# Zero-padded k^T scores, packed kv transposes, and q transposed by VectorE in a fused linear-attention and expert-attention kernel

## The chip, the cores and the metric

The kernel runs on one core of a Trainium2 chip. A core has a matrix engine (TensorE, PE in the profile, its weight loads shown as PEld), a vector engine (VectorE, DVE), a scalar engine (ScalarE, ACT), GpSimd (POOL) and an engine that here only issues transfers (SyncE, SP), beside 16 DMA engines. Each engine runs its own instructions in order and waits on semaphores. The metric is the device time of one execution in microseconds; lower is better.

## The reference

Two layers, batch 8, 8 heads, sequence 576, head size 64, all float32. The first is attention without softmax, and a norm over each head:

```python
kv = np.einsum('bhsd,bhse->bhde', k, v)
out = np.einsum('bhsd,bhde->bhse', q, kv)
rms = np.sqrt(np.mean(out * out, axis=-1, keepdims=True) + 1e-06)
out / rms * g_norm            # heads side by side give x: (8, 576, 512)
```

The second has four experts, each a causal softmax attention with head size 64; every token takes the two experts with the largest logits:

```python
logits = x @ w_gate           # two largest, softmax over the two -> w
for e in range(4):
    q, k, v = x @ wq[e], x @ wk[e], x @ wv[e]
    a = causal_softmax(q @ k.transpose(0, 2, 1) / 8)
    out += (w of e, where e is among the two) * (a @ v @ wo[e])
```

## The kernel before

Each batch passes through three generators, and a planner's loop (`merge`, L517) writes their pieces into one program in the order of estimated costs (`yield 4.3` and the like, with totals `CA, CX, CS`, L526).

**`stage_a(b)` (L191), the first layer.** `p_kv` gathers k^T v of all heads, two heads in the two halves of the partitions, over four blocks of 128 positions and a rest of 64. `kv_copy` writes it to `kvx` (the two heads beside each other, on the diagonal) and to `kv2` (the same as a full 128x128 block with zeros). `p_kt` transposes the four blocks of `kv2`; `p_kg` multiplies them with the gate weights (`wg_bd`), which gives four further columns of `kvx`, so that the logits come out beside the attention output. `q_block(i)` (L196) turns block i of q (128 positions, 8 heads) into `qT`, with four TensorE transposes into PSUM (`p_q`, L200) and one VectorE copy (L205); there are five blocks, the last with 64 positions. `p_out` (L242) then multiplies qT with kvx, block by block. VectorE copies it to `o_sb` (L249), ScalarE squares it (L253), VectorE sums the squares (L259). A chain of small VectorE operations makes the inverse root (L270 to L282), and POOL scales the rows into `x_tok` (L297).

**`stage_x(b)` (L307)** transposes x_tok on TensorE (`p_x`) and ScalarE copies it to `xT`.

**`stage_s(b)` (L323), the second layer.** VectorE makes the gates. `proj(pr)` makes q^T and k^T of two experts at a time, one in partitions 0 to 63, the other in 64 to 127 (`qTp` and `kT`, one ScalarE copy each, L384); `kT` rotates through three tiles whose columns 576 to 639 are zero. `scores(pr)` multiplies, for each block of keys and each of the two experts (`el`), the 64 rows of that expert (L400); ScalarE takes the exponential into `PT` (L410), POOL masks the diagonal blocks (L415). `pv(pr)` multiplies with v, `o_t` transposes, and `final` (L502) makes the output rows, which SyncE stores (L512). The order within the stage is a written string (L494 to L496).

**Order.** Stage A of batch 0 comes first, then stage X of 0 beside stage A of 1, then for each b stage S of b beside stage X of b+1 and stage A of b+2. The framework then orders each engine's instructions by this program order and by its own estimate of when operands are ready, so an instruction can move ahead of an earlier one that isn't ready.

**Loads.** `load_qkv` (L110) fetches one batch on SyncE's queue: k and v in runs of 1 KB, their rests and q in runs of 256 bytes; q comes last, one transfer per block (L134). Two batches fit (`bufs=2`). The weights (L158) pass through one staging tile and a VectorE scaling each (L159). Stores are on the same queue.

## Time and profile before

| | |
|---|---|
| time, median of 3 runs | 328.2 us (323.96 to 330.56) |
| the profiled execution's own time | 324.47 us |
| its span in the profile | 322.5 us |
| mean granted TensorE clock | 0.945 |
| busy: PE, DVE, ACT, POOL | 276.0, 189.2, 153.0, 79.5 us |
| DMA queue | 75248 packets, 39.86 MB, 47.1% of 16 engines' span |

Busy time of TensorE counts overlapping matmuls once; the ends of matmuls are modelled, so starts are the better measure of what one costs. A row of the groups names line, engine, operation, the tile written and those read, then for matmuls the active rows and columns of the array (64*128 is a matmul over 64 rows). The chain of work follows the last instruction back to what released it, step by step. A row of the stages gives the busy time of each engine between two times of the span. In the timeline a row is a run of like instructions: its start, its length to the end of the last one, and their number.

### The profile page before, as it was taken

The page shows a single profiled execution, that of the slowest core. Times are in us where ns is not written, and L with a number is a line of the kernel's source. Part 1 is how long each engine was busy: PE and PEld are TensorE (multiplying, and loading weights), DVE is VectorE, ACT ScalarE, POOL GpSimd, SP SyncE. Part 2 cuts the span into 40 slices and gives each one's busy share as a digit, 9 for nine tenths or more (in the row PEclk, how much of TensorE's full clock was granted, in tenths as well). Part 3 has the DMA queues.
Part 4 walks back from the last instruction along what each step waited for, and adds up shares of the span by engine and source line. Part 5 has one row for each costly group of instructions (what it writes and reads, how often), then busy time and mean ns, then how long its engine had stood idle before and what let it go on. Part 6 is the DMA issues. An engine that isn't in the chain of part 4 may idle for free.

```text
span 322.5 us, 6704 instructions
## 1 busy us (share of the span) xinstructions
PE 276.0 (86%) x2624; PEld 220.4 (68%) x2624; DVE 189.2 (59%) x537; ACT 153.0 (47%) x273; POOL 79.5 (25%) x148
## 2 busy tenths in 40 slices
PE   1675579799979997999889996999889996999984
PEld 1565468588858775887667875887667875867641
DVE  0249948846884568646775578546774578424130
ACT  0203123653464654545554554545555554585843
POOL 8100600441044110702053101612052101630210
PEclk9959599999999999799999999799999999899977
DMA  6977999999704269194608372001200120021124
GB/s 195 243 199 195 205 301 223 298 180 276 152 2 133 64 202 192 41 253 127 169 3 269 81 182 58 2 0 67 82 2 2 65 83 0 0 100 53 65 83 147
DMA packets 75280, 40.30 MB, mean 125 GB/s; under 512 B 54000, under 2 KB 70384, under 8 KB 75248
## 3 DMA queue, kind: packets, MB, share of 16 engines
q1 hardware_dynamic: 75248, 39.86, 47.1%
q8 instruction: 21, 0.34, 0.5%
q14 instruction: 11, 0.09, 0.1%
HBM read 30.42 MB, written 9.44 MB: 124 GB/s over the span
## 4 chain that ended last, share of the span: by engine, by line
PE 70%; DVE 10%; ACT 9%; SPq 4%; issue 3%; POOL 1%; DMA 1%; DVEq 0%; ACTq 0%; POOLq 0%
PE p_proj L373 11%; PE p_out L242 11%; PE p_v L355 7%; PE p_sc L400 7%; PE p_O L451 7%; PE p_y L506 6%; PE p_q L200 6%; PE p_x L313 6%; PE p_kv L179 5%; ACT PT L410 3%; PE p_kg L224 3%; DVE o_sb L249 3%; SPq L134 2%; PE p_OT L484 2%; POOL x_tok L297 1%
## 5 line engine op out<-in xcount | busy, mean ns | idle before, releaser
L415 POOL TENSOR_SCALAR_AFFINE_SELECT PT<-PT 128x256 bf16<-128x256 bf16 (+1 forms) x80 | 29.3, 381 | 143.4 <-ACT PT L410 143.4
L410 ACT ACTIVATE PT<-p_sc 128x576 bf16<-128x576 f32 (+3 forms) x80 | 53.9, 714 | 20.1 <-PE p_sc L400 18.1
L297 POOL TENSOR_TENSOR x_tok<-o_sb,y 128x512 f32<-128x512 f32 (+1 forms) x40 | 42.0, 1080 | 85.1 <-DVE y L280 85.0
L242 PE MATMUL p_out<-kvx,qT 128*128 128x136 f32 (+1 forms) x320 | 48.1, 292 | 0.0
L400 PE MATMUL p_sc<-qTp,kT 64*128 64x288 f32 (+2 forms) x192 | 35.7, 358 | 10.7 <-ACT PT L410 5.9
L242 PEld LDWEIGHTS p_out<-kvx,qT 128*128 128x128 f32 (+1 forms) x320 | 40.2, 181 | 4.8 <-ACT sq L253 2.1
L253 ACT ACTIVATE sq<-p_out 128x512 f32<-128x512 f32 (+1 forms) x40 | 23.8, 596 | 39.9 <-DVE o_sb L249 38.4
L318 ACT CAST xT<-p_x 128x512 fp32r<-128x512 f32 (+1 forms) x40 | 21.8, 545 | 34.3 <-PE p_x L313 34.3
L400 PEld LDWEIGHTS p_sc<-qTp,kT 64*128 64x128 f32 x192 | 19.8, 185 | 21.9 <-ACT PT L410 8.5
L179 PE MATMUL p_kv<-v_b,k_b 128*64 128x64 f32 x512 | 25.7, 260 | 10.3 <-DMA v_b<-in_v_dram 10.3
L249 DVE COPY o_sb<-p_out 128x544 f32<-128x544 f32 (+1 forms) x40 | 28.7, 719 | 7.7 <-PE p_out L242 7.2
L362 DVE CAST vext<-p_v 128x256 bf16<-128x256 f32 (+1 forms) x40 | 17.0, 425 | 26.3 <-PE p_v L355 25.6
L259 DVE TENSOR_REDUCE ms<-sq 128x8 f32<-128x520 f32 (+1 forms) x40 | 27.4, 688 | 7.9 <-ACT sq L253 7.8
L205 DVE COPY qT<-p_q 128x512 f32<-128x512 f32 (+1 forms) x40 | 24.7, 634 | 11.6 <-PE p_q L200 11.0
L451 PEld LDWEIGHTS <-PT 128*128 128x128 bf16 (+2 forms) x480 | 24.1, 103 | 10.8 <-issue 5.3
L179 PEld LDWEIGHTS p_kv<-v_b,k_b 128*64 128x64 f32 x512 | 23.0, 173 | 12.2 <-DMA k_b<-in_k_dram 6.7
L451 PE MATMUL p_O<-vext,PT 128*128 128x65 bf16 (+2 forms) x480 | 30.3, 199 | 0.4 <-ACT PT L410 0.4
L313 PE MATMUL p_x<-ident_f,x_tok 128*128 128x128 f32 (+1 forms) x160 | 25.9, 289 | 5.4 <-POOL x_tok L297 4.3
L355 PE MATMUL p_v<-wv_r,xT 128*128 128x256 f32 (+1 forms) x160 | 28.3, 300 | 0.7 <-ACT kv L188 0.7
L373 PE MATMUL p_proj<-xT,wk_r 128*128 128x288 f32 x128 | 24.3, 314 | 3.6 <-ACT qTp L384 3.6
L506 PE MATMUL p_y<-wo_b,OT 128*128 128x512 bf16 (+1 forms) x80 | 25.1, 417 | 0.7 <-ACT OT L489 0.7
L511 ACT COPY y<-p_y 128x512 f32<-128x512 f32 (+1 forms) x40 | 23.0, 595 | 5.0 <-PE p_y L506 2.7
(67 smaller groups left out, 360.9 us busy)
## 6 DMA issues: line engine op xcount, KB each, us to landing
q_b<-in_q_dram SPq DMA_DIRECT2D x32, 256.0 KB, 5.2
out_dram<-y SPq DMA_DIRECT2D x32, 256.0 KB, 2.1
k_b<-in_k_dram SPq DMA_DIRECT2D x7, 1024.0 KB, 6.0
v_b<-in_v_dram SPq DMA_DIRECT2D x7, 1024.0 KB, 10.2
k_b<-in_k_dram SPq DMA_DIRECT2D x4, 256.0 KB, 4.7
v_b<-in_v_dram SPq DMA_DIRECT2D x4, 256.0 KB, 4.9
k_rem<-in_k_dram SPq DMA_DIRECT2D x8, 128.0 KB, 9.2
v_rem<-in_v_dram SPq DMA_DIRECT2D x8, 128.0 KB, 7.5
```

Source lines behind the costliest of these rows:

```text
L179: nc.tensor.matmul(p_kv[hh * Dh : (hh + 1) * Dh, c, :], lhsT=lk, rhs=rv, start=(j == 0), stop=(j == NF), skip_group_check=True,)
L242: nc.tensor.matmul(p_o[:nt, c // 2, (c % 2) * 2 * GW : (c % 2 + 1) * 2 * GW], lhsT=qT[:, c, t0 : t0 + nt], rhs=kvb[:, c, :, :].rearrange(" ...
L249: nc.vector.tensor_copy(out=ob[:nt, i].rearrange("p (k h) g -> p k (h g)", k=2), in_=p_o[:nt, :, 0 : 4 * GW])
L297: nc.gpsimd.tensor_tensor(out=xt[:nt], in0=ob[:nt, i, :, 0:Dh], in1=y[:nt, i * H : (i + 1) * H].unsqueeze(2).to_broadcast([nt, H, Dh]), op ...
L313: nc.tensor.transpose(p_x[:, c, :nt], xts[i][:nt, 2 * c : 2 * c + 2, :].rearrange("p h d -> p (h d)"), ident_f[:nt, :nt],)
L355: nc.tensor.matmul(p_v[:nt, :], lhsT=xT[:, c, t0 : t0 + nt], rhs=w_r["v"][:, c, :, :].rearrange("p e f -> p (e f)"), start=(c == 0), stop= ...
L373: nc.tensor.matmul(p_p[:, s, 0:HALF], lhsT=w_r[nm][:, c, 2 * pr : 2 * pr + 2, :].rearrange("p e f -> p (e f)"), rhs=xT[:, c, s * HALF : (s ...
L400: nc.tensor.matmul(p_s[:, el, o : o + hi - lo], lhsT=kTp[pb, kb * P : (kb + 1) * P], rhs=qTp[pb, lo:hi], start=True, stop=True,)
L410: nc.scalar.activation(PT[:, :, d0 : d0 + o], p_s[:, :, 0:o], ACTF.Exp, scale=scale)
L415: nc.gpsimd.affine_select(out=d, in_=d, compare_op=AluOpType.is_ge, fill=0.0, base=0, pattern=[[0, 2], [1, w]], channel_multiplier=-1,)
L451: nc.tensor.matmul(p_O[:nq, bank, (2 * n + el) * (Hd + 1) : (2 * n + el + 1) * (Hd + 1)], lhsT=PT[:nk, el, col : col + nq], rhs=vx[:nk, kb ...
L506: nc.tensor.matmul(p_y[:nq, :], lhsT=OT[:, pr, s0 : s0 + nq], rhs=wo_b[:, pr, :], start=(pr == 0), stop=(pr == EP - 1),)
```

## The change

1. **Scores.** Each pair of experts gets two `kT` tiles instead of one, `kT{pr}{el}`. The 64 partitions of the other expert and the columns past 576 are set to zero once. ScalarE copies k^T in two pieces, one to each tile, and the score matmul runs over all 128 rows with the whole `qTp`. The tiles of a pair are used again in each batch.
2. **Packed kv.** ScalarE copies `p_kv` as it is to `kvc`, with four 64-column pieces side by side; two of them make one 128x128 transpose, so there are two transposes and two `p_kg` products a batch. `wg_bd` is laid out to match, loaded in four transfers, and the result goes to `kvx` in two copies.
3. **q.** The load puts 32 dimensions of one head on 32 partitions, each position's 32 values a run of 128 bytes: 16 transfers a batch instead of 5. Four VectorE transposes of 32x32 blocks, one for each pair of heads, then make `qT` at the start of stage A. `q_block` and `p_q` are gone.
4. **Start.** The weights come in the order q, k, v, staged in the buffers of x_tok; wo is staged in those of y. Stage X of batch 0 runs alone, stage S of 0 beside stage A of 1, then stage X of 1 beside stage A of 2; from batch 1 on the streams are as before. The load of batch 3 is issued after the first of these. The planner's totals and yields are changed.

```diff
-        t = const.tile([P, NCH, P], FP32, name=f"kv2_{j}")
-        nc.gpsimd.memset(t[:], 0.0)
-        kv2s.append(t)
+        t = const.tile([P, NCH, Dh], FP32, name=f"kvc{j}")
...
+    zrow = ysb.tile([P, NB * P], FP32, tag="zrow", name="zrow", bufs=1)
+    nc.gpsimd.memset(zrow[:], 0.0)
...
+    kTs = []
+    for pr in range(EP):
+        pair = []
+        for el in range(2):
+            t = const.tile([P, NB * P], FP32R, name=f"kT{pr}{el}")
+            other = slice((1 - el) * Hd, (2 - el) * Hd)
+            nc.vector.tensor_copy(out=t[other, :], in_=zrow[other, :])
+            nc.vector.tensor_copy(out=t[:, S : NB * P], in_=zrow[:, S : NB * P])
+            pair.append(t)
+        kTs.append(pair)
...
-        qt = qkvp.tile([P, NB, H, Dh], FP32, tag="q_b", name="q_b")
+        qt = qkvp.tile([P, NCH, S // 32, 32], FP32, tag="q_b", name="q_b")
...
-        for i, (t0, nt) in enumerate(blocks):
-            nc.sync.dma_start(
-                qt[:nt, i, :, :], q[b, :, t0 : t0 + nt, :].rearrange("h p d -> p h d")
-            )
+        for c in range(NCH):
+            for hh in range(2):
+                for dh in range(2):
+                    p0 = (2 * hh + dh) * 32
+                    nc.sync.dma_start(
+                        qt[p0 : p0 + 32, c, :, :],
+                        q[b, 2 * c + hh, :, dh * 32 : (dh + 1) * 32].rearrange("(g p) d -> p g d", p=32),
+                    )
         return qt, kt, vt
...
-    wg_st = const.tile([P, NCH, E], FP32, name="wg_st")
-    nc.sync.dma_start(wg_st[:], moe_w_gate.rearrange("(c p) e -> p c e", p=P))
-    wg_bd = const.tile([P, NCH, 2, E], FP32, name="wg_bd")
+    wg_st = const.tile([P, EP, 2, E], FP32, name="wg_st")
+    for c2 in range(2):
+        for m in range(EP):
+            h0 = 4 * m + 2 * c2
+            nc.sync.dma_start(
+                wg_st[c2 * Dh : (c2 + 1) * Dh, m, :, :],
+                moe_w_gate[h0 * Dh : (h0 + 2) * Dh, :].rearrange("(a d) e -> d a e", d=Dh),
+            )
+    wg_bd = const.tile([P, EP, 2, 2, E], FP32, name="wg_bd")
     nc.gpsimd.memset(wg_bd[:], 0.0)
-    for hh in range(2):
-        pp = slice(hh * Dh, (hh + 1) * Dh)
+    for c2 in range(2):
+        pp = slice(c2 * Dh, (c2 + 1) * Dh)
         nc.vector.tensor_scalar_mul(
-            out=wg_bd[pp, :, hh, :], in0=wg_st[pp], scalar1=g_wide[pp]
+            out=wg_bd[pp, :, c2, :, :], in0=wg_st[pp], scalar1=g_wide[pp]
         )
     w_r = {}
-    for name, wdram in (("v", moe_wv), ("q", moe_wq), ("k", moe_wk)):
+    for name, wdram in (("q", moe_wq), ("k", moe_wk), ("v", moe_wv)):
         wr = const.tile([P, NCH, E, Hd], FP32R, name=f"w{name}_r")
-        wf = wst.tile([P, NCH, E, Hd], FP32, name="w_stage", tag="w_stage")
-        for e in range(E):
-            nc.sync.dma_start(wf[:, :, e, :], wdram[e].rearrange("(c p) f -> p c f", p=P))
-        nc.vector.tensor_scalar_mul(
-            out=wr[:].rearrange("p c e f -> p (c e f)"),
-            in0=wf[:].rearrange("p c e f -> p (c e f)"),
-            scalar1=g_wide[:],
-        )
+        for c0 in range(0, NCH, 2):
+            wf = blk.tile([P, 2, E, Hd], FP32, tag="x_tok", name="w_stage", bufs=NB + 1)
+            for c in range(2):
+                nc.sync.dma_start(
+                    wf[:, c, :, :],
+                    wdram[:, (c0 + c) * P : (c0 + c + 1) * P, :].rearrange("e p f -> p e f"),
+                )
+            nc.vector.tensor_scalar_mul(
+                out=wr[:, c0 : c0 + 2].rearrange("p c e f -> p (c e f)"),
+                in0=wf[:].rearrange("p c e f -> p (c e f)"),
+                scalar1=g_wide[:],
+            )
         w_r[name] = wr
     loads[1] = load_qkv(1)
-    wo_st = wst.tile([P, EP, D], FP32, name="wo_st", tag="w_stage")
+    wo_b = const.tile([P, EP, D], BF16, name="wo_b")
     for pr in range(EP):
-        nc.sync.dma_start(
-            wo_st[:, pr, :], moe_wo[2 * pr : 2 * pr + 2].rearrange("two d m -> (two d) m")
-        )
-    wo_b = const.tile([P, EP, D], BF16, name="wo_b")
-    nc.vector.tensor_copy(out=wo_b[:], in_=wo_st[:])
+        wo_st = ysb.tile([P, D], FP32, tag="y", name="wo_st")
+        nc.sync.dma_start(wo_st[:], moe_wo[2 * pr : 2 * pr + 2].rearrange("two d m -> (two d) m"))
+        nc.vector.tensor_copy(out=wo_b[:, pr, :], in_=wo_st[:])
...
-    def kv_copy(p_kv, kvb, kv2):
+    def kv_copy(p_kv, kvb, kvc):
+        nc.scalar.copy(kvc[:], p_kv[:])
         for hh in range(2):
             pp = slice(hh * Dh, (hh + 1) * Dh)
             nc.vector.tensor_copy(out=kvb[pp, :, hh, 0:Dh], in_=p_kv[pp, :, :])
-            nc.scalar.copy(kv2[pp, :, hh * Dh : (hh + 1) * Dh], p_kv[pp, :, :])
     def stage_a(b, res):
         qb, kb, vb = loads[b]
         qT = s1.tile([P, NCH, S], FP32, tag="qT", name="qT", bufs=1)
-        kvb, kv2 = kvx[b % 2], kv2s[b % 2]
-        def q_block(i):
-            t0, nt = blocks[i]
-            p_q = small([P, NCH, P], "p_q")
-            for c in range(NCH):
-                nc.tensor.transpose(
-                    p_q[:, c, :nt],
-                    qb[:nt, i, 2 * c : 2 * c + 2, :].rearrange("p h d -> p (h d)"),
-                    ident_f[:nt, :nt],
-                )
-            nc.vector.tensor_copy(out=qT[:, :, t0 : t0 + nt], in_=p_q[:, :, :nt])
+        kvb, kvc = kvx[b % 2], kvcs[b % 2]
+        for c in range(NCH):
+            nc.vector.transpose(qT[:, c, :], qb[:, c, :, :].rearrange("p g d -> p (g d)"))
         p_kv = small([P, NCH, Dh], "p_kv")
         for c in range(NCH):
             kv_pair(p_kv, c, kb, vb, kr[b % 2], vr[b % 2])
-        kv_copy(p_kv, kvb, kv2)
-        yield 4.3
-        q_block(0)
-        yield 0.5
-        p_kt = small([P, NCH, P], "p_kt")
-        for c in range(NCH):
-            nc.tensor.transpose(p_kt[:, c, :], kv2[:, c, :], ident_f[:])
-        kt_sb = s1.tile([P, NCH, P], FP32, tag="kvT", name="kvT")
+        kv_copy(p_kv, kvb, kvc)
+        yield 3.5
+        p_kt = small([P, EP, P], "p_kt")
+        for m in range(EP):
+            nc.tensor.transpose(
+                p_kt[:, m, :], kvc[:, 2 * m : 2 * m + 2, :].rearrange("p c e -> p (c e)"), ident_f[:]
+            )
+        kt_sb = s1.tile([P, EP, P], FP32, tag="kvT", name="kvT")
         nc.vector.tensor_copy(out=kt_sb[:], in_=p_kt[:])
-        yield 0.5
-        q_block(1)
-        yield 0.5
-        p_kg = small([P, NCH, 2, E], "p_kg")
-        for c in range(NCH):
+        yield 0.22
+        p_kg = small([P, EP, 2, 2, E], "p_kg")
+        for m in range(EP):
             nc.tensor.matmul(
-                p_kg[:, c, :, :].rearrange("p a e -> p (a e)"),
-                lhsT=kt_sb[:, c, :],
-                rhs=wg_bd[:, c, :, :].rearrange("p a e -> p (a e)"),
+                p_kg[:, m].rearrange("p c a e -> p (c a e)"),
+                lhsT=kt_sb[:, m, :],
+                rhs=wg_bd[:, m].rearrange("p c a e -> p (c a e)"),
                 start=True,
                 stop=True,
             )
-        nc.vector.tensor_copy(out=kvb[:, :, :, Dh:GW], in_=p_kg[:])
-        yield 0.9
-        for i in range(2, NB):
-            q_block(i)
-            yield 0.5
+        for hh in range(2):
+            pp = slice(hh * Dh, (hh + 1) * Dh)
+            nc.vector.tensor_copy(
+                out=kvb[pp, :, hh, Dh:GW].rearrange("p (m c) e -> p m c e", m=EP), in_=p_kg[pp, :, :, hh, :]
+            )
+        yield 0.45
...
                 if nm == "q":
                     t = moe.tile([P, S], FP32R, tag="qTp", name="qTp", bufs=3)
+                    nc.scalar.copy(
+                        t[:].rearrange("p (s n) -> p s n", s=2), p_p[:, :, 0:HALF]
+                    )
+                    out_t.append(t)
                 else:
-                    t = kTs[(2 * b + pr) % 3]
-                nc.scalar.copy(
-                    t[:, 0:S].rearrange("p (s n) -> p s n", s=2), p_p[:, :, 0:HALF]
-                )
-                out_t.append(t)
+                    for el in range(2):
+                        pb = slice(el * Hd, (el + 1) * Hd)
+                        nc.scalar.copy(
+                            kTs[pr][el][pb, 0:S].rearrange("p (s n) -> p s n", s=2), p_p[pb, :, 0:HALF]
+                        )
                 yield 1.0
         def scores(pr):
-            qTp, kTp = res["qk", pr]
+            (qTp,) = res["qk", pr]
             PT = res["PT", pr] = moe.tile([P, 2, strips], BF16, tag="PT", name="PT", bufs=3)
             def piece(parts):
@@ -396,11 +410,10 @@
                 o = 0
                 for kb, lo, hi in parts:
                     for el in range(2):
-                        pb = slice(el * Hd, (el + 1) * Hd)
                         nc.tensor.matmul(
                             p_s[:, el, o : o + hi - lo],
-                            lhsT=kTp[pb, kb * P : (kb + 1) * P],
-                            rhs=qTp[pb, lo:hi],
+                            lhsT=kTs[pr][el][:, kb * P : (kb + 1) * P],
+                            rhs=qTp[:, lo:hi],
                             start=True,
                             stop=True,
                         )
@@ -523,20 +536,26 @@
             except StopIteration:
                 live.remove(x)
-    CA, CX, CS = 11.8, 2.25, 14.5
+    CA, CX, CS = 8.8, 2.25, 15.0
     res = [dict() for _ in range(B)]
     merge((stage_a(0, res[0]), CA, 0.0, 1.0))
     loads[2] = load_qkv(2)
-    merge((stage_x(res[0]), CX, 0.3, 0.6), (stage_a(1, res[1]), CA, 0.0, 1.0))
+    merge((stage_x(res[0]), CX, 0.0, 1.0))
     y_gen = None
     for b in range(B):
-        if b + 3 < B:
+        if 0 < b < B - 3:
             loads[b + 3] = load_qkv(b + 3)
-        merge(
-            (stage_s(b, res[b], y_gen), CS, 0.0, 1.0),
-            (stage_x(res[b + 1]) if b + 1 < B else None, CX, 0.05, 0.4),
-            (stage_a(b + 2, res[b + 2]) if b + 2 < B else None, CA, 0.1, 1.0),
-        )
+        streams = [(stage_s(b, res[b], y_gen), CS, 0.0, 1.0)]
+        if b == 0:
+            merge(streams[0], (stage_a(1, res[1]), CA, 0.1, 0.8))
+            loads[3] = load_qkv(3)
+            merge((stage_x(res[1]), CX, 0.2, 1.0), (stage_a(2, res[2]), CA, 0.0, 0.6))
+        else:
+            if b + 1 < B:
+                streams.append((stage_x(res[b + 1]), CX, 0.05, 0.4))
+            if b + 2 < B:
+                streams.append((stage_a(b + 2, res[b + 2]), CA, 0.1, 1.0))
+            merge(*streams)
         y_gen = final(b, res[b]["OT"])
     for _ in y_gen:
         pass
```

## The prediction

> **What bounds the kernel now.** I read the profile in this order: busy shares, chain, the stages, then TensorE's own timeline inside one batch.
>
> First the page's busy line, its granted clock and DMA busy share by fortieths of the span (tenths), and the two lines of the chain that ended last.
>
> ```profile
> PE 276.0 (86%) x2624; PEld 220.4 (68%) x2624; DVE 189.2 (59%) x537; ACT 153.0 (47%) x273; POOL 79.5 (25%) x148
> ...
> PEclk9959599999999999799999999799999999899977
> DMA  6977999999704269194608372001200120021124
> ...
> PE 70%; DVE 10%; ACT 9%; SPq 4%; issue 3%; POOL 1%; DMA 1%; DVEq 0%; ACTq 0%; POOLq 0%
> PE p_proj L373 11%; PE p_out L242 11%; PE p_v L355 7%; PE p_sc L400 7%; PE p_O L451 7%; PE p_y L506 6%; PE p_q L200 6%; PE p_x L313 6%; PE p_kv L179 5%; ACT PT L410 3%; PE p_kg L224 3%; DVE o_sb L249 3%; SPq L134 2%; PE p_OT L484 2%; POOL x_tok L297 1%
> ```
>
> TensorE holds 70% of the chain. Of that the change touches p_q (6%, 19 us), p_kg (3%, 9 us) and p_sc (7%, 23 us). Next the stages: three of the start, and one steady batch.
>
> ```profile
> 0.00:20.00 20.00, 8.48 (x96) 7.21 (x97) 3.50 (x10) 2.02 (x3) 8.42 (x28) 0.94 0.86 206
> 20.00:40.00 20.00, 13.11 (x97) 11.39 (x99) 16.53 (x41) 4.29 (x8) 5.01 (x5) 0.67 0.84 209
> 40.00:62.00 22.00, 18.30 (x172) 15.57 (x168) 15.42 (x34) 9.35 (x17) 1.80 (x4) 0.96 1.10 269
> ...
> 201.00:237.00 36.00, 33.81 (x328) 27.67 (x328) 22.50 (x64) 18.09 (x34) 8.45 (x15) 0.95 0.10 34
> ```
>
> Columns after the length: busy us of PE, PEld, DVE, ACT, POOL, then clock, DMA share, GB/s. A steady batch takes 36 us and TensorE is busy in 33.8 of them: it is the bound there, with DVE at 63%. The first 62 us are different: TensorE is idle for 22 us, DMA is saturated (0.84 to 1.10), and the clock falls to 0.67. So **work taken from TensorE pays in the steady batches, and nearly nothing in the first 55 us**, where loads and the chain of the first batch decide. S(0)'s first projection starts only at 55.47 us.
>
> Last, TensorE's timeline in that batch, around single score matmuls and around the q transposes.
>
> ```profile
> 208.05 0.52 PE L355 MATMUL p_v<-wv_r,xT 128*128 128x256 f32 x3
> 208.40 0.43 PE L373 MATMUL p_proj<-xT,wq_r 128*128 128x288 f32 x2
> 208.76 0.35 PE L400 MATMUL p_sc<-qTp,kT 64*128 64x192 f32 x1
> 209.04 0.74 PE L355 MATMUL p_v<-wv_r,xT 128*128 128x256 f32 x4
> ```
> ```profile
> 216.70 1.06 PE L224 MATMUL p_kg<-wg_bd,kvT 128*128 128x8 f32 x8
> 217.69 0.60 PE L400 MATMUL p_sc<-qTp,kT 64*128 64x288 f32 x3
> ...
> 220.23 1.04 PE L200 MATMUL p_q<-ident_f,q_b 128*128 128x128 f32 x8
> 221.10 0.41 PE L451 MATMUL p_O<-vext,PT 128*128 128x65 bf16 x8
> ```
>
> Starts, not durations, tell the price, since matmuls overlap. Eight q transposes take 220.23 to 221.10, 0.109 us each. p_proj's 288 columns cost 0.13 us each in a run, p_v's three 0.117 (208.05 to 208.40). But from the last p_proj (about 208.53) through one visit of 64-row score matmuls to p_v's second start (209.26 in the trace) is 0.73 us; p_proj and p_v account for 0.25 of it. **A visit to the 64-row form costs 0.48 us**, though the two matmuls of a pair start within 0.005 us of each other. Planned order makes some nine visits a batch.
>
> **The change, part by part (steady batch).**
>
> *q transposes off TensorE.* 4 per block, 5 blocks: 20 x 0.107 (the group's share of the stream in two batches) = 2.1 us, plus one exit from the 64-row last block, 0.2: **-2.3 us**.
>
> *Packed kv.* p_kt 4 to 2: 2 x 0.109 = 0.2. p_kg 8 to 4 records: 4 x 0.112 = 0.45. **-0.65 us**.
>
> *Padded scores.* 24 matmuls a batch now take 4.8 us of the stream, 1.1 of it waiting for ACT, so 3.7. As 128-row matmuls: 288 columns twice at 0.133, 320 at 0.146, 448 at 0.20 (from 288 by columns), 192 and 64 at the weight load's 0.112; 0.83 per head, x4 = 3.3: -0.4. The matmul behind a visit starts 0.1 to 0.2 late, nine times: 0.9 to 1.8, but p_v behind p_proj at 207.82 also lost 0.1 to a semaphore, with no change of form. So from -0.9 to -2.2; I take **-1.5 us**.
>
> *What TensorE's saving meets.* Sum -4.45 us a batch. Against it: the k^T copy on ScalarE becomes two of 64x576. Partitions don't shorten a copy (64x256 0.366, 128x256 0.373), so +0.64 each, twice a batch; TensorE already waits there (kT: 4.7 us in the run). v_proj covers the first, nothing sure the second. ScalarE goes from 18.1 to about 19 us of 32. I charge 1.0 us a batch (bounds 0 and 2.5): **net -3.5**.
>
> *VectorE.* Gone: 4 x 0.687 + 0.425 = 3.2 us a batch, and kvT halves (-0.25). Added: 4 transposes of 128x576 f32 and one copy of 0.19. The trace has no such transpose. Bounds: 0.42 (the 128x1024 scaling's 0.75, by elements) and 1.3 (the slow scaling of wk_r, whole); I take 0.75, by the 128x512 copy's 0.687: 3.0 us, so about even, 22.5 us of 32. At 1.3 it is 24.7 of 32, worth perhaps 1 us a batch to the net. They stand ahead of the kv copies on VectorE's in-order queue, so a late q holds kvx, vext and inv behind it.
>
> *Loads.* q becomes 16 transfers of 576 runs of 128 B instead of 5 of 256 B: 9216 packets for 4608 a batch. In the trace a packet took 21.2 ns at 256 B, 52.5 at 1 KiB, 94.8 at 2 KiB; the line through the first two gives 16 ns at 128 B. Bounds: 10 (what a 4 B packet took) and 52.5 (no cheaper than 1 KiB), -0.3 and +24 us a batch; I take 16, by the nearest row, 256 B: 9216 x 16 / 16 engines = 9.2 us against 6.1, +3.1 a batch. A batch's other traffic is (2048 x 52.5 + 1024 x 21.2 + 576 x 94.8) / 16 = 11.5, so 20.7 us of a 32 us batch. Issuing costs SyncE 0.6 each, so 9.6 instead of about 3.5; q of batch 6 is issued at 150 to 158 and used at 214, so 50 us of cover hide both. Without it, each late load costs 3 us.
>
> The page "DMA: Bandwidth & Descriptors", section "Why small descriptors are slow", of the Trainium skill counts 3 cycles a packet beside the data, 11 for 256 B, so by it 128 B needs 7 of those 11; q would then cost 7.8 us instead of my 9.2, which would move the start by 1.4 us.
>
> The same skill speaks against the padding: "TensorE: Matmul & The Clock Gate", Part 3, wants small contractions sliced onto row groups so that they run side by side. The pairs here do (starts 0.005 us apart). By that rule alone padding would add 12 x 0.13 = 1.6 us a batch, 13 us in all, in place of my gain; the 0.48 us visits are why I go by the row.
>
> *The start.* The chain before: w_gate's load, p_kg at 19.21, p_q 2.42 us, p_out at 23.47. q ends 3.1 later, w_gate's loads are 4 issues instead of 1 (+1.8), p_q's 2.4 and half of p_kg go: p_out near 25. With the chain behind it as long as now (x_tok 34.99, five of 1.13 on POOL, then the copy), S(0) can start near 44 instead of 55.5. But A(1), done by 55.5 before, is now inside S(0): kv 3.6, kt and kg 0.7, p_out 5.1 = 9.4 us, so 53. X(1) and A(2) then run without a score stage beside: POOL's 5.65 us and VectorE's 1.4 per block against 1.0 on TensorE leave about 3 us open, and q(1) comes up to 2 late. **+2.5 us**, bounds -6 and +8. Kernel constants (zero rows, 8 copies) lie under the first loads.
>
> *Sum.* Six batches carry an A beside an S: 6 x -3.5 = -21. The last two have only the scores: 2 x -1.5 = -3. Start +2.5. Span 322.5 - 21.5 = 301; the profiled execution took 324.47, 2.0 over its span, so 303. It is 1.1% under the median 328.2 (323.96 to 330.56), so I say **304**.
>
> **The rivals.**
>
> *Stalls eat it.* TensorE drops below what VectorE and ScalarE need with their waits: net -1.5 a batch, start +5: 322.5 - 9 - 2 + 5 + 2 = 318. For it: ms, o_sb, sq chains are already at 63%, and transposes may cost 1.3. Against: in the last two batches, with no A beside them, TensorE is still busy 41.6 of 48.5 us (274 to 322.5).
>
> *The start gains.* If S(0) starts at 44 and TensorE fills, with no wait for q(1), and the full 4.45 come through: 322.5 - 27 - 3 - 5 + 2 = 290.
>
> *The loads become the bound: slower.* Place: SyncE's ring, first four batches, q last in each. Load period equals 32 us when 0.576 x ns + 11.5 = 32, at 36 ns a packet; it loses the whole gain near 45. At 45 a load without output is 34 us, eight are 272, weights 8, and after the last one some 60 us of S(5) to S(7): 340. For it: DMA share is 0.8 to 1.1 up to 94 us, and the run count doubles. Against: smaller packets were cheaper at every size seen.
>
> *It doesn't do what it says.* The scores keep paying since p_x's 64-row block and p_O's forms still switch: only q and kv gain; 6 x -2.2 + 3.5: about 313, inside the first rival's ground.
>
> **How the numbers follow.** Forecast 0.60, stalls (with the unswitched scores) 0.20, start gains 0.10, loads 0.10. Unknown terms alone give 288 to 318 round 304. Range 288 to 321: it takes in the stalls and leaves out most of the loads' case and the best of the start's. A change under 2% can't be told from none here (the three runs lie 2% apart). Faster by over 2% (below 321.6): forecast nearly whole, start 0.10, two thirds of the stalls: 0.80; within 2% 0.09; slower 0.11.
>
> **What will show it.** Right: no p_q, p_sc groups as 128*128 at 0.11 to 0.15 us between starts, a steady batch of 31 to 33 us, DVE rows of about 0.75 for qT, first p_proj near 44 us, 128 B packets below 25 ns. Wrong: kvx or vext waiting for a DMA of q_b; DMA share near 1 past 100 us; p_sc starting 0.2 us after a change of form as now; kT waits above 10 us; transposes over 1 us.

## The result, and the profile after

The changed kernel takes **386.1 us** (median of four runs, 384.9 to 387.3) against 329.0 for the kernel before in the same comparison (324.0 to 330.6). Executions of one kernel differ by 2 to 3% with the granted clock, so ratios here are of the fast ones alone (386.1 to 326.1: 1.184, 95% interval 1.170 to 1.199), while times are medians of all, between which I don't read differences under 3 us. It is 18% slower where I forecast 304 us and 7% faster. The profiled execution took 387.31 us, with a span of 385.6.

The page of the changed kernel, busy times, then granted clock and DMA share by fortieths of the span:

```profile
PE 286.6 (74%) x2402; PEld 225.8 (59%) x2416; DVE 186.3 (48%) x546; ACT 160.2 (42%) x281; POOL 78.8 (20%) x146
...
PEclk9998597598999999558996569986699866999997
DMA  7959898966900200003880039700397002202033
```

TensorE is busy 74% of the span in place of 86%, its clock is below 0.9 in 18 of the 40 slices (7 before), and past the first 110 us DMA is far from full. The batches, from one p_kv to the next (length; busy us of PE, PEld, DVE, ACT, POOL; clock; DMA share; GB/s):

```profile
147.10:195.50 48.40, 36.99 (x296) 28.66 (x298) 22.22 (x66) 18.69 (x34) 8.20 (x15) 0.79 0.29 67
195.50:244.10 48.60, 37.72 (x303) 29.55 (x304) 22.74 (x66) 19.59 (x36) 8.86 (x16) 0.79 0.45 104
244.10:291.70 47.60, 36.71 (x301) 28.82 (x302) 22.77 (x66) 19.48 (x36) 8.73 (x16) 0.82 0.40 98
```

A steady batch takes 48 us in place of 36, at a clock of 0.8. The first projection starts at 44.8 us, as forecast (44). Of the 63 us that the span is longer, 17 lie before the fifth p_kv (147.1 us against 130.3), 36 in these three batches and 10 behind them. TensorE's timeline inside one batch shows how it is lost:

```profile
252.05 0.63 PE L323 MATMUL p_x<-ident_f,x_tok 128*128 128x128 f32 x4 [0.61 <-DVE vext L372]
253.36 0.74 PE L365 MATMUL p_v<-wv_r,xT 128*128 128x256 f32 x4 [0.67 <-ACT xT L328]
254.71 0.63 PE L323 MATMUL p_x<-ident_f,x_tok 128*128 128x128 f32 x4 [0.61 <-DVE vext L372]
256.01 0.74 PE L365 MATMUL p_v<-wv_r,xT 128*128 128x256 f32 x4 [0.68 <-ACT xT L328]
```

p_x and p_v alternate, and each waits for the copy that empties the tile of the other, 2.65 us a round. They share the pool of small PSUM tiles, which has two banks. In the addresses of the built program both take turns in one bank here; in the kernel before they alternate between the two. The other bank is held by the last of the previous batch's five p_y tiles. Its matmuls are done at 234 us:

```profile
233.61 0.59 PE L519 MATMUL p_y<-wo_b,OT 128*64 128x512 bf16 x2
```

and ScalarE empties it 40 us later. Its copies to y in this stretch (the run at 273.76 begins with that 64-row copy):

```profile
232.14 0.62 ACT L524 COPY y<-p_y 128x512 f32<-128x512 f32 x1
233.48 0.59 ACT L524 COPY y<-p_y 128x512 f32<-128x512 f32 x1 [0.18 <-ACT OT L502]
273.76 1.05 ACT L524 COPY y<-p_y 64x512 f32<-64x512 f32 x2
```

The copy needs a buffer of y. There are four for five tiles a batch, and the four stores are on SyncE behind the next load:

```profile
228.65 1.08 SPq L128 DMA_DIRECT2D k_rem<-in_k_dram  x1
229.79 1.83 SPq L128 DMA_DIRECT2D v_rem<-in_v_dram  x1
231.71 12.75 SPq L144 DMA_DIRECT2D q_b<-in_q_dram  x16
244.57 30.30 SPq L525 DMA_DIRECT2D out_dram<-y  x5
274.96 0.54 SPq L122 DMA_DIRECT2D k_b<-in_k_dram  x1
```

The tiles are ready at 226 to 234 us, but SyncE issues 16 q transfers in 12.75 us first, and the next load stands behind the fifth store in turn. SyncE's waits for y copies, 156.9 us before the change, are 203.5 us now. The stores of the four land by 250, so for the 24 us after that the copy waits only for its place in ScalarE's order. I take it that the order was made for a store that comes late; that part is argued, not shown.

### The profile page after: what moved, and what is told of

Same layout as the page of the kernel before. It is cut to its first block, busy times and chain, and to the rows that moved or that the text cites. A ratio compares the mean times of both kernels' runs of the same rounds, so it can differ in the third digit from the quotient of the medians.

```text
span 385.6 us, 6408 instructions
## 1 busy us (share of the span) xinstructions
PE 286.6 (74%) x2402; PEld 225.8 (59%) x2416; DVE 186.3 (48%) x546; ACT 160.2 (42%) x281; POOL 78.8 (20%) x146
## 5 line engine op out<-in xcount | busy, mean ns | idle before, releaser
L252 PE MATMUL p_out<-kvx,qT 128*128 128x136 f32 (+1 forms) x320 | 60.9, 344 | 8.4 <-ACT PT L423 3.5
L413 PE MATMUL p_sc<-qTp,kT 128*128 128x288 f32 (+2 forms) x192 | 51.4, 364 | 16.0 <-DVE osc L485 5.8
L252 PEld LDWEIGHTS p_out<-kvx,qT 128*128 128x128 f32 (+1 forms) x320 | 51.1, 227 | 17.6 <-ACT PT L423 7.7
L307 POOL TENSOR_TENSOR x_tok<-o_sb,y 128x512 f32<-128x512 f32 (+1 forms) x40 | 41.6, 1071 | 67.3 <-DVE y L290 67.3
L413 PEld LDWEIGHTS p_sc<-qTp,kT 128*128 128x128 f32 x192 | 32.7, 209 | 25.7 <-ACT kT L399 9.6
L323 PE MATMUL p_x<-ident_f,x_tok 128*128 128x128 f32 (+1 forms) x160 | 28.8, 319 | 18.3 <-POOL x_tok L307 9.9
L365 PE MATMUL p_v<-wv_r,xT 128*128 128x256 f32 (+1 forms) x160 | 30.2, 321 | 10.0 <-ACT xT L328 7.2
L480 DVE RECIPROCAL inv<-p_O 128x6 f32<-128x6 f32 (+2 forms) x48 | 8.2, 171 | 60.2 <-PE p_O L464 60.2
L372 DVE CAST vext<-p_v 128x256 bf16<-128x256 f32 (+1 forms) x40 | 16.9, 424 | 41.8 <-PE p_v L365 41.6
L323 PEld LDWEIGHTS p_x<-ident_f,x_tok 128*128 128x128 f32 (+1 forms) x160 | 19.8, 168 | 27.3 <-issue 13.8
L365 PEld LDWEIGHTS p_v<-wv_r,xT 128*128 128x128 f32 (+1 forms) x160 | 22.6, 193 | 16.1 <-ACT xT L328 10.8
L199 PE MATMUL p_kv<-v_b,k_b 128*64 128x64 f32 x512 | 22.5, 237 | 7.7 <-DMA v_b<-in_v_dram 7.5
```

What stands on the lines that cost most here:

```text
L199: nc.tensor.matmul(p_kv[hh * Dh : (hh + 1) * Dh, c, :], lhsT=lk, rhs=rv, start=(j == 0), stop=(j == NF), skip_group_check=True,)
L252: nc.tensor.matmul(p_o[:nt, c // 2, (c % 2) * 2 * GW : (c % 2 + 1) * 2 * GW], lhsT=qT[:, c, t0 : t0 + nt], rhs=kvb[:, c, :, :].rearrange(" ...
L307: nc.gpsimd.tensor_tensor(out=xt[:nt], in0=ob[:nt, i, :, 0:Dh], in1=y[:nt, i * H : (i + 1) * H].unsqueeze(2).to_broadcast([nt, H, Dh]), op ...
L323: nc.tensor.transpose(p_x[:, c, :nt], xts[i][:nt, 2 * c : 2 * c + 2, :].rearrange("p h d -> p (h d)"), ident_f[:nt, :nt],)
L365: nc.tensor.matmul(p_v[:nt, :], lhsT=xT[:, c, t0 : t0 + nt], rhs=w_r["v"][:, c, :, :].rearrange("p e f -> p (e f)"), start=(c == 0), stop= ...
L413: nc.tensor.matmul(p_s[:, el, o : o + hi - lo], lhsT=kTs[pr][el][:, kb * P : (kb + 1) * P], rhs=qTp[:, lo:hi], start=True, stop=True,)
```

## The experiments

"Theory q" below is that one: the q part (128-byte loads and VectorE transposes) makes the loss, through stores, y buffers and the bank. Times are medians of four runs (five for the new q path alone); the kernel before took 325.3 to 328.3 in these comparisons.

**A fifth y buffer.**
```diff
-    ysb = ctx.enter_context(tc.tile_pool(name="ysb", bufs=4))
+    ysb = ctx.enter_context(tc.tile_pool(name="ysb", bufs=5))
```


> The changed kernel with five buffers for the output rows instead of four, nothing else. Theory Q (queue): the stores of a batch stand on SyncE's queue behind the next load's 16 q transfers, so the fifth output row block finds no free buffer, its matrix product keeps one of the two small PSUM banks for some 40 us, and p_x, p_v, p_kt and p_kg of the next batch pass through the other bank one by one. With a fifth buffer the steady batch falls from 48 us to 31 to 33 us and the time to 300 to 312 us. Rival P (parts): the padded scores, the VectorE transposes or the 128-byte loads cost the time themselves; then the time stays above 370 us.

348.6 us (346.2 to 350.3). The small tiles use both banks in turn again, and 37.5 us come back: less than theory Q expected, far more than theory P. The bank is shown as the larger part, but 20 us over the kernel before stay.

**Stores on ScalarE's queue**, four buffers.
```diff
-            nc.sync.dma_start(out[b, s0 : s0 + nq, :], y[:nq, :])
+            nc.scalar.dma_start(out[b, s0 : s0 + nq, :], y[:nq, :])
```


> The changed kernel with its four buffers, but the 40 stores are issued on ScalarE's queue instead of SyncE's. Theory Q: the stores no longer wait behind the q loads, so the bank is free in time: 302 to 320 us, less good than a fifth buffer by the ScalarE time of 40 issues (0.3 to 0.5 us each). If the number of buffers alone mattered and not the place in the queue, it stays near 386 us. Rival P: above 370 us.

339.7 us (335.6 to 346.9). Taking the stores from behind the q transfers frees the bank as well as the buffer does (the fifth copy to y comes about 1 us after its matmuls), and again a rest stays, above what theory Q expected. Why it is 9 us below the run with the fifth buffer is not followed up.

**The old q path, the rest of the change kept** (five buffers).
```diff
-            nc.vector.transpose(qT[:, c, :], qb[:, c, :, :].rearrange("p g d -> p (g d)"))
+        def q_block(i):
...
```


> As the run with five buffers, but q is loaded and transposed as in the kernel before (5 transfers of 256-byte runs a batch, 20 TensorE transposes and 5 VectorE copies). The engines' orders are the same with four buffers and with five here. Theory Q: no bank is held; the time lies above the run with five buffers by the price of p_q, 2.3 us a batch: 315 to 326 us. Rival P, if the q part is innocent: as bad as the changed kernel, above 370 us.

316.8 us, ratio 0.970 (0.961 to 0.980): without its q part the change is faster, by 2 to 4%.

**Only the new q path** on the kernel before (its load and its transposes, four buffers).
```diff
-        def q_block(i):
...
+            nc.vector.transpose(qT[:, c, :], qb[:, c, :, :].rearrange("p g d -> p (g d)"))
```


> The kernel before with the q part of the change alone (16 transfers of 128-byte runs a batch, VectorE transposes, no p_q), four buffers for the output. Theory Q: the q part alone brings the fault: one bank held, a steady batch of 45 us or more, 360 to 390 us. Rival P, if padded scores or the start are to blame: 305 to 325 us.

358.2 us, ratio 1.090. The q part makes the loss alone. The second cost is seen in the run with five buffers. VectorE's timeline there:

```profile
191.26 0.77 DVE L217 STREAM_TRANSPOSE qT<-q_b 128x576 f32<-128x576 f32 x1
...
197.12 0.78 DVE L217 STREAM_TRANSPOSE qT<-q_b 128x576 f32<-128x576 f32 x1
200.88 0.20 DVE L480 RECIPROCAL inv<-p_O 128x6 f32<-128x6 f32 x1 [2.98 <-PE p_O L464]
...
204.11 0.28 DVE L485 TENSOR_TENSOR osc<-p_O,inv 64x128 bf16<-64x128 f32 x1
204.32 1.42 DVE L217 STREAM_TRANSPOSE qT<-q_b 128x576 f32<-128x576 f32 x2
```

q of this batch was issued at 137 to 149 us and had long landed; the last two transposes simply stand behind the scaling of p_O. TensorE meanwhile:

```profile
198.65 0.50 PE L252 MATMUL p_out<-kvx,qT 128*128 128x136 f32 x2
199.77 0.40 PE L464 MATMUL p_O<-vext,PT 128*128 128x65 bf16 x8 [0.63 <-ACT PT L423]
...
201.92 1.17 PE L464 MATMUL p_O<-vext,PT 128*128 128x65 bf16 x18 [1.08 <-DVE osc L485]
204.54 0.87 PE L413 MATMUL p_sc<-qTp,kT 128*128 128x320 f32 x2 [1.45 <-DVE osc L485]
206.21 3.99 PE L252 MATMUL p_out<-kvx,qT 128*128 128x136 f32 x16 [0.79 <-ACT PT L423]
```

By the program's addresses two p_out tiles are opened with their first chunks and hold two of the three large PSUM tiles from 197 to 210 us; p_sc and p_O pass through the third one by one, each waiting for the other's reader.

**The last chunk first**, five buffers: p_out can't begin before the fourth transpose.
```diff
-            for c in range(NCH):
+            for c in reversed(range(NCH)):
                 nc.tensor.matmul(
```


> The changed kernel with five output buffers and one more edit: stage A's p_out loop takes the chunks of q^T in the order 3, 2, 1, 0 instead of 0 to 3. The transposes still come in the order 0 to 3, so a p_out tile is now begun only when all four chunks are there. Before this edit (348.6 us) the order of the program opens three p_out tiles with the first one or two chunks, and they hold two of the three pairs of PSUM banks while VectorE has the later transposes behind other work. Theory half-open tiles: the steady batch goes from 38.6 to 34 to 35.5 us, and the second batch's p_out no longer stops at 62 us; 320 to 333 us in all. Theory late loads (all that is left is that loads come later in the first 100 us): no change, 345 to 350 us.

324.2 us (317.8 at a granted clock of 0.977, the others 323.4 to 325.5 at 0.94 to 0.95), 24.4 us less by the order of one loop. Steady batches fall from 38.6 to 33.9 us. Half-open tiles are shown as the second cost.

**The same with four buffers.**


> The changed kernel with the last chunk first alone, four output buffers. The one PSUM bank stays held by the fifth output tile. If the two harms add up, the 24 us that this order gave with five buffers come off the 386: 358 to 366 us. If TensorE waits for the held bank anyway, so that the half-open p_out tiles lie beside it: 378 to 387 us.

357.7 us: 28.4 less than the change, and 33.5 more than with five buffers. The two costs add, to within some 4 us.

**Runs of 256 bytes**, 16 transfers as before.
```diff
-                        qt[p0 : p0 + 32, c, :, :],
-                        q[b, 2 * c + hh, :, dh * 32 : (dh + 1) * 32].rearrange("(g p) d -> p g d", p=32),
+                        qt[p0 : p0 + 32, c, :, :].rearrange("p (g e) d -> p g (e d)", e=2),
+                        q[b, 2 * c + hh, dh * (S // 2) : (dh + 1) * (S // 2), :].rearrange("(g p) d -> p g d", p=32),
```


> The kernel of the run before (five output buffers, last chunk first) with q still in 16 transfers a batch, but each of 288 runs of 256 bytes in place of 576 runs of 128 bytes: half of the rows of a head in place of half of its columns. It leaves out the right placing of q (the scores of the gates are of a shuffled q); the work of every engine is the same. Theory packets: the loads of the start come every 15 to 16 us in place of every 19, and the time is 6 to 15 us below the run before. Theory number of transfers (SyncE needs some 0.75 us for each): the loads keep their 19 us, and the time is within 3 us of the run before.

321.1 us (317.2 to 324.1), 3 below: not to be told from the run before. The loads of the start come every 17.6 to 18.7 us in place of 18.0 to 20.3 (15.9 and 13.7 with the old path, before its loads wait for buffers). In the traces the fifth p_kv comes at 136.3 us, 2.0 earlier, and every later batch is 2.0 earlier too; with the old path it comes at 128.9. So the size of the packets is the smaller part of it, and the number of transfers, or their shape, is left with the rest.

**The first two batches' q on ScalarE's queue.**
```diff
+        qeng = nc.scalar if b < 2 else nc.sync
...
-                    nc.sync.dma_start(
+                    qeng.dma_start(
```


> The changed kernel with five output buffers and the last chunk first (324.2 us), and the q transfers of batches 0 and 1 issued on ScalarE's queue, those of the later batches on SyncE's as before. In that run the fifth batch's p_kv begins at 138.3 us against 128.9 with the old q path, and the steady batches and the tail are as short as with it: all of what is left lies in the start. Theory issues (32 transfers keep SyncE from issuing what stands behind them): the weights and batch 1's k and v come 10 to 20 us earlier, 314 to 319 us. Theory bytes and packets (the DMA engines are the limit there): 322 to 326 us.

350.5 us. Both theories missed: ScalarE runs its instructions in order and issues these 32 transfers from 0.8 to 55.5 us; the first copy of kv stands behind them and comes at 56.8 us.

```profile
ACT L206 <- DMA q_b<-in_q_dram: 55.5, 1, 55.5
PEld p_kt L226 <- ACT kvc L206: 41.2, 1, 41.2
```

The Trainium skill, "DMA: Bandwidth & Descriptors", section "Issuing engines are not separate DMA queues", says that issuing from several engines only saves the sequencer's issue time. In this run the two queues moved 180 to 236 GB/s over the first 56 us, against 177 to 202 on SyncE's queue alone in the run with the last chunk first. But the compute engine behind the full queue waits, here 55.5 us, and that costs far more.

**Only the packed kv transposes** (four buffers).
```diff
-        for c in range(NCH):
-            nc.tensor.transpose(p_kt[:, c, :], kv2[:, c, :], ident_f[:])
+        for m in range(EP):
+            nc.tensor.transpose(
+                p_kt[:, m, :], kvc[:, 2 * m : 2 * m + 2, :].rearrange("p c e -> p (c e)"), ident_f[:]
+            )
```


> Of the change only the packed kv transposes (with its load of the gate weights and the order of the weight loads): q, scores and the streams of the first batches as before, four output buffers. My forecast gave the packing 0.65 us a batch, some 4 to 5 us in all: 322 to 325 us. By the runs with the old q path, where leaving out the padding or the new start changed nothing, the packing is what made them faster: 315 to 319 us.

317.0 us, ratio 0.973 (0.964 to 0.982), with steady batches of 34.2 to 35.2 us. The fifth p_kv comes at 130.1 us, as before (130.3), so the order of the weight loads, which this run has too, is not what saves. **Old q with old scores**, and **old q with the old merging of the first batches**:
```diff
-                            lhsT=kTs[pr][el][:, kb * P : (kb + 1) * P],
-                            rhs=qTp[:, lo:hi],
+                            lhsT=kTp[pb, kb * P : (kb + 1) * P],
+                            rhs=qTp[pb, lo:hi],
```


> Old q path, old scores of 64 rows, five output buffers; of the change only the packed kv transposes and the new start are left. The same with padded scores took 316.8 us. My forecast gave the padded scores 1.5 us a batch, 12 us in all: 327 to 331 us. If the switches of the form cost nothing (theory row groups side by side are the better form), padding costs 0.13 us a matmul pair, and this run is at 303 to 312 us.


```diff
-    merge((stage_x(res[0]), CX, 0.0, 1.0))
...
+    merge((stage_x(res[0]), CX, 0.3, 0.6), (stage_a(1, res[1]), CA, 0.0, 1.0))
```


> Old q path, five output buffers, padded scores and packed kv, and the streams of the first batches merged as before the change. With the new start it took 316.8 us. My forecast charged the new start +2.5 us (bounds -6 and +8): 311 to 323 us, 314 by the estimate. If the earlier second layer of batch 0 is what saves, 322 to 330 us.

317.5 and 315.9 us, level with 316.8; the first is inside neither of its two ranges. Neither the padding nor the new start is worth anything measurable; the packing is the whole gain.

**Only the new q path, both mends** (five buffers, last chunk first).


> The kernel before with the new q path alone, five output buffers and the last chunk first; without the two mends it took 358.2 us. If the q transposes' 2.1 us a batch come through once nothing is held: 312 to 322 us. If, as between the two runs with and without the new q path (33.9 against 34.4 us a steady batch, 9 us more in the start), the start eats what the steady batches gain: 326 to 336 us.

350.3 us, well above both theories; the mends gave 8 us. With the old kv transposes the order on TensorE differs, and p_out waits 2.79 us for the same late transposes:

```profile
198.80 1.18 PE L439 MATMUL p_O<-vext,PT 128*128 128x65 bf16 x18 [1.19 <-DVE osc L460]
202.77 1.47 PE L230 MATMUL p_out<-kvx,qT 128*128 128x136 f32 x5 [2.79 <-DVE qT L201]
```

**q ahead of k and v** in the loads, three runs: alone, with both mends from batch 3 on, and on the kernel of the run above.
```diff
+        if b > 0:
+            load_q()
         for h0 in range(0, H, step):
             main(kt, k, h0, h0 + step)
```


> The changed kernel with one edit: from batch 1 on, the 16 q transfers of a batch are issued ahead of its k and v, not behind them; four output buffers and the chunks in their order. Theory order (the program's order on the engines is made as if q came last, so the transposes stand late on VectorE, p_out tiles are opened half and the fifth output tile keeps its bank): the order made for this kernel has whole p_out tiles and both small PSUM banks in turn, so steady batches of 33 to 35 us and 318 to 334 us in all. Theory queue (stores wait behind 16 transfers and four buffers are too few, whatever the order): batches of 42 us or more, 350 to 386 us.

> The changed kernel with five output buffers, the last chunk first, and from batch 3 on q ahead of k and v. The start is that of the run with the last chunk first (fifth p_kv at 138.3 us). If the transposes still came late there, the steady batch goes from 33.9 to 32 to 33 us: 313 to 320 us. If TensorE's idle time there has other causes: 321 to 326 us.

> The kernel before with the new q path alone, five output buffers, the last chunk first, and from batch 3 on q ahead of k and v; without this last edit it took 350.3 us at some 40 us a steady batch, where p_out waits 2.8 us for the last two transposes, which stand behind the scaling of p_O on VectorE. Theory late transposes: the steady batch comes to 34 to 36 us and the time to 320 to 332 us. Theory that four-chunk kv transposes and the new q path don't go together for another reason: 343 to 352 us.

340.1, 340.1 and 337.9 us. The first is the telling one: four buffers, chunks in their order, and yet 46 us less, with whole p_out tiles, and with both banks in turn for p_x and p_v, although SyncE carries the same transfers. The fifth y copy still comes late there, 16 us after its matmuls:

```profile
204.19 0.62 PE L525 MATMUL p_y<-wo_b,OT 128*64 128x512 bf16 x2
220.53 0.57 ACT L530 COPY y<-p_y 64x512 f32<-64x512 f32 x1
```

In the change it comes 40 us after (in the kernel before, within 1 us) and covers the stretch in which p_x and p_v need both banks; here it comes before all but the first of them. So the theory of the queue alone falls: four buffers and 16 transfers make the copy late, and the order made for the program, which follows where q stands in the load, decides how late and what the held bank then stops. The half-open tiles come from that order. But none of the three reaches the expected time: in the new order the projections come ahead of p_kv and no longer fill the pauses between p_x and p_v (VectorE waits 43.8 us for p_v in the second run, 17.4 with the fifth buffer alone), and a steady batch takes 37.6 us. In the third run 12 of the 25 us over the kernel before go; the rest is open.

**Old q for batches 0 to 2**, new q after it: ahead of k and v, behind them, and with one chunk of four ahead.
```diff
+    MIX = 3
...
+        if b < MIX:
+            qt = qkvp.tile([P, NB, H, Dh], FP32, tag="q_b", name="q_b")
+        else:
+            qt = qkvp.tile([P, NCH, S // 32, 32], FP32, tag="q_b", name="q_b")
```


> Padded scores, packed kv and the new start, five output buffers; q of batches 0 to 2 loaded and transposed as before the change, that of batches 3 to 7 in 128-byte runs ahead of k and v and transposed on VectorE. Theory start: the loads of the start are as short as with the old q path (fifth p_kv near 129 us) and the steady batches 32.5 to 34 us in place of 34.4: 306 to 314 us. If the 128-byte loads of batches 3 to 5 come late in their turn: 316 to 324 us.

> As the run with the old q path for batches 0 to 2 (333.2 us, 37.6 us a steady batch), but with the 128-byte transfers of batches 3 to 7 behind k and v as in the change, and the last chunk first. The order on TensorE is then that of the run with the last chunk first. Theory start (the loads of the first batches are the third cost, 9 us): fifth p_kv at 129 to 131 us, steady batches of 33.9 us: 311 to 316 us, level with or a little below the old q path alone (316.8). If the start is not to blame: 320 to 326 us as with the new q path throughout.

> The run before with one of the four chunks of q ahead of k and v and three behind them; the same work. Only the order of the program changes by it. If the steady batch hangs on the order alone, not on the work, it moves by over 0.5 us from 33.9 (between 32 and 37 us): 305 to 312 or 319 to 330 us. If all four chunks ahead cost 37.6 us because of late k and v on the chip, one chunk costs a quarter of it: 34.8 us, 316 to 320 us.

333.2, 319.4 and 316.3 us. The first, with the 37.6 us batches of the order above, is outside both of its ranges, and so is the second. In the second the fifth p_kv is at 134.5 us: of the 9 us between 138.3 (new q) and 128.9 (old q) less than half goes, so the loads of the first batches are shown as a part of the third cost only; the rest is open. The third has 33.7 us a batch, inside neither theory's range for the batch; its time fits the second, but 37.6 is not reached by quarters, so it decides nothing.

No version beats 316 us by more than the measurement tells; old q with packed kv (315.9 to 317.5 in four variants) stays the best, 3% below the kernel before.

## Why the prediction was wrong, point by point

The chain, in medians: 386.1 as changed; 348.6 once the bank is free; 324.2 once p_out tiles are whole; 316.8 with the old q path. Of the q part's 69 us, 37.5 are the held bank and 24.4 the half-open tiles (28.4 when taken off first). The 7.5 left are not a firm size: the runs behind 324.2 reach from 317.8, one us above the old path, to 325.5. In the traces (323.4 and 315.6 us) the difference lies in the start, before the fifth p_kv.

- **The step that failed** is "q of batch 6 is issued at 150 to 158 and used at 214, so 50 us of cover hide both". The cover was there for the data: with five buffers q lies 40 us in SBUF before its first transpose. What has no cover stands behind the 16 transfers on SyncE: the stores, then the buffers of y, then ScalarE's copy, then a PSUM bank, held for 40 us a batch. I counted the queue's 9.6 us (12.75 measured) and asked only whether q comes in time, not who is queued behind it. The signs that I had named for being wrong stayed out (no wait of kvx or vext for q_b, kT waits of 9.6 us in all, transposes of 0.76 us): they watched q's data and the parts, not the stores.
- **"They stand ahead of the kv copies on VectorE's in-order queue"** failed too. I read the position from the source. In the program all four stand behind the kv copies, the last ones behind the scaling of p_O too, and the first of them still opens a p_out tile. My worry, that a late q would hold VectorE, is the reverse of what happened.
- **q transposes off TensorE** (-2.3 us a batch): the size was right and worth little. In one steady batch each, old path, then new:

```profile
163.30:197.80 34.50, 32.59 (x325) 26.57 (x324) 23.31 (x68) 19.52 (x36) 8.88 (x16) 1.00 0.52 138
```
```profile
172.30:206.30 34.00, 30.23 (x305) 23.92 (x304) 22.18 (x67) 19.69 (x36) 8.92 (x16) 1.00 0.61 142
```

  TensorE is busy 2.4 us less and the batch is 0.5 us shorter: idle time took the place of the work. That is my stalls rival, which I gave 0.20; the charge of 1.0 us for stalls should have been about 2. With both mends the whole change's steady batch is 33.9 us against 36.3 before: 2.4 of the 3.5 us that I forecast.
- **Packed kv** (-0.65 us a batch) was mis-sized: 36.3 to 34.6 us on average, and some 8 us in all by its own run (325.3 to 317.0). The matmuls removed account for half (p_kg from 0.99 to 0.35 us of TensorE's stream in one batch, p_kt from 0.44 to 0.22); the other half is a sum of waits that moved, and I have not separated them.
- **Padded scores** (-1.5) brought nothing. TensorE is even 0.65 us a batch busier with them (32.6 against 31.95). The price of a visit to the 64-row form, 0.48 us, was read from one place; what I multiplied by nine was a late start of 0.1 to 0.2 us behind each visit, most of the 1.5, and the run without padding doesn't show it. Weighing it, I left the rule of the Trainium skill ("TensorE: Matmul & The Clock Gate", Part 3: small contractions side by side on row groups), by which padding would cost 1.6 us a batch, by the prediction's estimate. The busy time has 0.65 of it, the time none.
- **VectorE** at 0.75 us a transpose: 0.763 measured, and its busy time a batch falls from 23.3 to 22.2 us where I said about even. **Packets** of 128 bytes at 16 ns: the busy time of the DMA engines differs by 12.9 us over eight batches between the runs with 128 and 256 bytes, 1.6 us a batch, which with 21.2 ns for 256 bytes gives 13.4 ns (in the trace of the change they took 13.65 on average), so q costs 7.7 us a batch, near the 7.8 by the page that I cited there and below my 9.2. I feared the packet, which is worth some 2 us; what stands behind the 16 transfers, and the order made around them, was what cost.
- **The start** (+2.5, with q in it): the first projection came when forecast, the fifth p_kv 9 us later with the new q than with the old; the new merging alone changes nothing.
- **The sums.** 303 us for the profiled execution, raised by 1.1%, is 306 and not 304; the last rival's 313 lacks the 2 us that the other sums add. Neither matters beside 386.
- **The rivals.** The one that I put on the other side, loads as the bound at 340 us, had the right edit and the right engine, SyncE's 16 transfers, but at the wrong price: DMA share is 0.29 to 0.45 in the steady batches. None asked what else uses that queue. So the 0.11 that I gave to slower was not this mechanism.

## What to carry to other kernels

When an edit multiplies the issues on a queue, list all that is queued behind them and follow each to the buffer and the PSUM bank that it frees; the data of the edit itself may have ample cover. When work moves to another engine, don't take its place there from the source: an order made by estimates can put it last, and a tile opened with the first piece of it holds its bank until the last. Taking work from the busiest engine pays only as far as the waits between the engines let it: here 2.4 us of matmuls gave 0.5.

## What the hardware showed that I had not expected

A loose stretch on TensorE is paid twice. In the run with the new q path alone and both mends, the stretches around the 2.79 us gap:

```profile
190.00:196.00 6.00, 6.00 (x46) 4.80 (x44) 2.65 (x5) 3.05 (x7) 0.64 (x2) 1.00 0.21 34
196.00:202.70 6.70, 2.79 (x37) 1.93 (x36) 3.69 (x12) 2.37 (x4) 0.81 (x2) 0.91 0.21 79
202.70:207.00 4.30, 4.23 (x17) 3.74 (x18) 0.97 (x2) 1.19 (x2) 0.41 (x1) 0.50 0.00 0
207.00:212.00 5.00, 5.00 (x24) 3.67 (x24) 1.93 (x4) 2.19 (x4) 0.65 (x2) 0.53 0.14 52
212.00:218.00 6.00, 5.80 (x61) 4.55 (x59) 4.75 (x13) 2.73 (x5) 0.00 (x0) 1.00 0.41 107
```

After a stretch busy to 42%, the clock is half for 9 us, in which TensorE is busy throughout: some 4.5 us more, on top of the gap. In the changed kernel no such gap is needed: the alternation of p_x and p_v leaves TensorE busy in 3.80 of 7 us with no pause over 0.7 us, and the clock falls as well.

```profile
249.00:256.00 7.00, 3.80 (x22) 2.76 (x22) 1.28 (x3) 3.31 (x6) 0.41 (x1) 1.00 0.01 3
256.00:262.00 6.00, 3.89 (x18) 2.73 (x18) 1.95 (x4) 0.37 (x1) 0.00 (x0) 0.62 0.00 0
262.00:270.00 8.00, 6.47 (x45) 4.95 (x45) 1.95 (x6) 1.57 (x2) 0.41 (x1) 0.65 0.00 0
```

The Trainium skill, "TensorE: Matmul & The Clock Gate", section "HAM oscillation — how this bites in real kernels", puts the rule as no idle gaps over some 3.4 us. Here gaps under 0.7 us were enough: a low share of busy time stands ahead of both drops, 42% and 54%. The share alone is not the rule either. In the kernel before, from 41.6 to 45.0 us, TensorE is busy for 1.76 of 3.40 us (52%) and the clock stays at 1.00.
